# Splitting a crossbar transpose and reordering the steps of a fused attention and mixer kernel

## The chip, the cores and the metric

The kernel runs on one core of a Trainium2 chip. The metric is the device time of one execution in microseconds (us). A run is called slow when it took over 1.5% longer than the fastest of its kernel. A difference of up to 2% is called "same".

Engines are named as the profile names them: PE is TensorE (matmuls), PEld its weight loads, DVE is VectorE, ACT is ScalarE, POOL is GpSimd, SP is SyncE, which here only issues transfers.

## The reference, cut to what matters

Eight batches, eight heads, 576 positions, head size 64. Causal attention with a decay bias comes first. Its output x (batch, 576, 512) goes through a low-rank mixer over positions and a two-layer network over channels:

```python
scores = scale * q @ k.T + minimum(bias, 0)        # causal; bias from a cumulative sum of s
x  = softmax(scores) @ v                           # heads side by side: (8, 576, 512)
u  = x + ((x.T @ U) @ V).T                         # rank 32, over positions
out = u + relu(u @ w_ch1) @ w_ch2                  # 512 -> 2048 -> 512, each token alone
```

## The kernel before

Work is written down as strings of short tokens, played in order. Each engine gets its own instructions in that order, and they wait for one another by semaphores. Heads go in pairs; four pairs make a batch. Tokens are cut into nine groups of 512, which don't line up with the batches of 576 positions. Thus group 2 of the tokens needs the mixed x of pair 11, the last pair of batch 2.

The tokens that the argument needs:

| token | what it does |
|---|---|
| `F`, `e` | one feed step: four 512-column matmuls of the channel network (`e` only from pair 16 on); `r` runs what follows them on ACT or DVE |
| `D` `E` / `d` `f` `m` | score matmuls of a head / their exponentials on ACT |
| `A`, `a` | value matmuls of a head / division on DVE, which yields x |
| `x` | crossbar transpose of the x of one pair (SP) |
| `Y`, `y` | mixer matmuls of one pair / addition of turned x, on DVE, which yields uT, the input of the network |
| `G` | one vector transpose (DVE) of four heads' q or k; the second and the fourth of a head group also issue four copies to the score slots (SP) |
| `W` | crossbar transpose of u of token group 0; later groups are turned inside their feed steps |
| `p`, `Z` | filler matmuls on PE / memsets on DVE (`Z1`: of the third score slot) |
| `k0 v0 s0 ...` in LOADS | the first loads, in order of issue: a mask (`k`), v of a batch (`v`), q and k of heads (`s`, `q`), U and V of the mixer (`u0`, `u1`), pieces of w_ch1 (`w`) and of w_ch2 (`x`) |

A suffix such as `x-2@1` means: the step for the pair two back, only in pairs whose number is 1 modulo 4.

```python
    def turn_group(g):                   # token G
        ...
        nc.vector.transpose(turned[:, e, c]..., src[:, c]...)
        if c == 1:
            for a in range(4):
                nc.sync.dma_start(out=slots[...], in_=turned[...])      # "slot<-turned"

    def turn_x(n):                       # token x
        nc.sync.dma_start_transpose(
            out=xT[n % 3], in_=x_of[n // PB][:, n % PB].rearrange("p t c -> p (t c)"))

    def turn_u(g):                       # one transfer, 16 blocks of 128 columns
        nc.sync.dma_start_transpose(
            out=u_sb[g % 2].rearrange("p d i c -> p (d i) c"),
            in_=uT[:, g % 4].rearrange("p d c -> p (d c)"))

    def mix_done(copy, n):               # token y: "uT L461"
        ...
                    nc.vector.tensor_add(dst, got[:, p - lo : e - lo], turned[:, p:e])

    PAIR = (                             # played once for each pair from 8 on
        "G1 F U-1@1 F r F D0 uA-1@1 Y-5@1 r D1 e d0 Y-4@2 r r x-3@0 G1 E1 yA-5@2 l0 yA-4@2 d1 "
        "A-2 x-2@0 yV-5@1 k0 k1 A-1 e E0 Y-3@2 Y-4@1 f1 a-2 m1 e r f0 x-2@2 r F a-1 x-2@1 K0 r "
        "yA-3@2 m0 ")
```

Two lists stand beside this: `SEQ`, the steps up to pair 7 (here "the preamble"), and `BANKS`, the PSUM bank of each tile in order.

The softmax here doesn't subtract the row's maximum and nothing guards it: scores larger than these inputs give would overflow.

## Time and profile before

| what | before | where it is read |
|---|---|---|
| time, median (lowest to highest) | 376.36 us (375.08 to 378.12), 4 runs | the runs |
| span of the profiled execution | 373.5 us (time 375.49) | page |
| first feed step | 36.39 us | PE's timeline |
| first scores of pair 8 | 79.7 us | PE's timeline |
| idle of PE in 0 to 45, 45 to 80, 80 to 140 us | 5.05, 0.26, 7.63 us | summed over PE's timeline |
| DVE waiting for turned x | 9.4 us | waits by engine |

### The profile page before, as it was taken

To read this page: it belongs to the slowest core of one execution; us is meant where nothing else is said; L and a number is where in the kernel's file an instruction comes from. 1 tells how busy PE (TensorE), PEld (TensorE's weight loads), DVE (VectorE), ACT (ScalarE), POOL (GpSimd) and SP (SyncE) were. 2 spreads that over 40 slices of the span, in tenths; PEclk is the share of its full clock that TensorE was granted. 3 is DMA by queue.
4 is the path that set the end of the run, shared out by engine and by line. 5 is a ranking of instruction groups with operands and counts; after the bars stand their busy time and mean duration, and the time that the engine had idled before them with its cause. 6 is when DMAs were issued, how large, how long until landed. Compare 5 with 4: busy or idle time off the path is not lost.

```text
span 373.5 us, 7658 instructions
## 1 busy us (share of the span) xinstructions
PE 355.2 (95%) x2968; PEld 197.3 (53%) x3014; DVE 192.5 (52%) x410; ACT 206.9 (55%) x397; POOL 108.4 (29%) x177
## 2 busy tenths in 40 slices
PE   8898999998999499999999999999999999999995
PEld 4567565445565265555555555555554444444443
DVE  7689776665878365677547555744333111011011
ACT  7799894078664188546853677448812611612610
POOL 8838464546356356474090000000000000000000
PEclk9999999999999699999999999999999999999999
DMA  7999999999999999999999731371033203203102
GB/s 91 176 202 167 172 136 163 193 214 212 149 153 177 169 177 143 156 200 175 172 137 137 175 79 35 109 165 34 2 79 90 54 28 104 38 28 113 29 31 82
DMA packets 113979, 46.16 MB, mean 124 GB/s; under 512 B 98272, under 2 KB 105824, under 8 KB 113944
## 3 DMA queue, kind: packets, MB, share of 16 engines
q0 software_dynamic: 65760, 18.54, 60.7%
q1 hardware_dynamic: 48184, 27.14, 37.7%
q8 instruction: 23, 0.38, 0.5%
q14 instruction: 12, 0.10, 0.1%
HBM read 37.73 MB, written 10.03 MB: 128 GB/s over the span
## 4 chain that ended last, share of the span: by engine, by line
PE 77%; DMA 9%; DVE 7%; ACT 3%; issue 2%; SPq 1%; DVEq 0%
PE pwork L480 30%; PE pwork L500 30%; PE pscore L265 9%; PE pwork L344 5%; DMA slot<-turned 4%; DVE slot L236 3%; DMA stage<-x_sb 2%; DMA slot<-rows_hbm 2%; PE pwork L440 2%; ACT slot L236 1%; SPq L256 1%; DVE x_sb L360 1%; ACT pT L330 1%; DVE slot L573 1%; PE pwork L375 1%
## 5 line engine op out<-in xcount | busy, mean ns | idle before, releaser
L480 PE MATMUL pwork<-uT,w_sb 128*128 128x512 bf16 x552 | 132.8, 381 | 6.4 <-DVE uT L461 5.3
L330 ACT ACTIVATE pT<-pscore 128x512 bf16<-128x512 f32 (+1 forms) x224 | 110.5, 567 | 50.8 <-PE pscore L265 45.8
L487 ACT ACTIVATE hT<-pwork 128x512 bf16<-128x512 f32 x144 | 86.6, 606 | 83.0 <-PE pwork L480 80.7
L500 PE MATMUL pwork<-w_sb,hT 128*128 128x512 bf16 (+2 forms) x573 | 129.0, 373 | 1.6 <-DVE o_sb L513 0.6
L480 PEld LDWEIGHTS <-w_sb 128*128 128x128 bf16 x576 | 54.4, 98 | 64.8 <-issue 7.4
L500 PEld LDWEIGHTS <-hT 128*128 128x128 bf16 x592 | 55.6, 98 | 61.7 <-issue 1.9
L513 DVE TENSOR_TENSOR o_sb<-pwork,stage 128x512 f32<-128x512 f32 (+2 forms) x37 | 24.9, 674 | 98.0 <-PE pwork L500 94.8
L265 PE MATMUL pscore<-slot 128*128 128x128 bf16 (+4 forms) x576 | 63.0, 242 | 4.3 <-DVE slot L236 1.7
L265 PEld LDWEIGHTS <-slot 128*128 128x128 bf16 x576 | 41.1, 99 | 27.5 <-issue 4.3
L250 DVE STREAM_TRANSPOSE turned<-qk_sd 128x576 bf16<-128x576 bf16 x48 | 52.8, 1130 | 4.4 <-DMA qk_sd<-in_k_dram 4.0
L333 DVE TENSOR_TENSOR pT<-pT,keep 128x512 bf16<-128x512 bf16 (+1 forms) x84 | 28.3, 349 | 26.8 <-ACT pT L330 26.7
L138 POOL DMA_DIRECT2D qk_sd<-in_k_dram x48 | 27.1, 567 | 43.7 <-DMA v_slot<-in_v_dram 21.8
L461 DVE TENSOR_TENSOR uT<-pwork,stage 128x448 bf16<-128x448 f32 (+7 forms) x56 | 22.8, 448 | 31.5 <-PE pwork L440 22.1
L344 PE MATMUL pwork<-v_slot,pT 128*128 128x65 bf16 x960 | 35.0, 194 | 0.3 <-DVE uT L461 0.3
L138 POOL DMA_DIRECT2D qk_sd<-in_q_dram x48 | 27.2, 577 | 27.2 <-DVE uT L461 11.1
L344 PEld LDWEIGHTS <-pT 128*128 128x128 bf16 x960 | 33.5, 98 | 2.9 <-issue 0.6
L360 DVE TENSOR_TENSOR x_sb<-pwork,rec 128x320 bf16<-128x320 f32 x64 | 31.5, 491 | 2.2
L146 POOL DMA_DIRECT2D v_slot<-in_v_dram x32 | 28.2, 890 | 6.6 <-DMA qk_sd<-in_q_dram 2.6
L236 DVE COPY slot<-pwork 64x576 bf16<-64x576 bf16 x20 | 15.6, 797 | 4.3 <-PE pwork L224 3.9
L359 DVE RECIPROCAL rec<-pwork 128x5 f32<-128x5 f32 x64 | 11.8, 185 | 6.6 <-PE pwork L344 6.5
L440 PE MATMUL pwork<-V_sb,z_sb 128*128 128x64 bf16 (+7 forms) x63 | 12.6, 284 | 0.1
L560 PE MATMUL pwork<-warm 128*128 128x512 bf16 x34 | 10.3, 443 | 1.4 <-DVE warm L116 1.3
(77 smaller groups left out, 107.4 us busy)
## 6 DMA issues: line engine op xcount, KB each, us to landing
out_dram<-o_sb SPq DMA_DIRECT2D x35, 256.0 KB
slot<-turned SPq DMA_DIRECT2D x96, 72.0 KB
v_slot<-in_v_dram POOLq DMA_DIRECT2D x32, 128.0 KB, 7.9
w_sb<-in_moe_w_ch_dram POOLq DMA_DIRECT2D x8, 512.0 KB, 10.5
qk_sd<-in_q_dram POOLq DMA_DIRECT2D x48, 72.0 KB, 9.4
qk_sd<-in_k_dram POOLq DMA_DIRECT2D x48, 72.0 KB, 7.2
stage<-in_q_dram POOLq DMA_DIRECT2D x2, 288.0 KB, 8.6
stage<-in_k_dram POOLq DMA_DIRECT2D x2, 288.0 KB, 9.3
```

The source lines that it names most:

```text
L138: nc.gpsimd.dma_start(out=qk_t[g][ds(32 * a, 32), c, :].rearrange("p (n f) -> p n f", n=6), in_=src[g // 2, 4 * (g % 2) + a].rearrange("(n ...
L146: nc.gpsimd.dma_start(out=vt[:, t, :, 0:D], in_=v[b, :, ds(t * 128, 128), :].rearrange("h p d -> p h d"),)
L236: copy(dst[:, :, :, :, par], tp_of[h][par * D : par * D + D].rearrange("p c t m -> p c m t"),)
L250: nc.vector.transpose(turned[:, e, c].rearrange("p (n m t) -> p n t m", n=6, t=3), src[:, c].rearrange("p (n t e d) -> p e n t d", n=6, t= ...
L265: nc.tensor.matmul(dst, lhsT=head_of(h)[:, ds(S + j * 128, 128)], rhs=head_of(h)[:, lo:hi], start=start, stop=stop and not bias, skip_grou ...
L330: nc.scalar.activation(dst, src, EXP, scale=scale)
L333: nc.vector.tensor_tensor(p, p, m, op=ALU.min)
L344: nc.tensor.matmul(po[:, i, :], lhsT=p_of(h)[:, ds(spot(j, i), 128)], rhs=v_slots[h // H % 3][:, j, h % H, :], start=(j == 0), stop=(j == ...
L360: nc.vector.tensor_tensor(x_of[b][:, h % H // 2, :, ts(h % 2, D)], po[:, :, 0:D], rec.to_broadcast([128, 5, D]), op=ALU.mult,)
L480: nc.tensor.matmul(f1, lhsT=w1_sb[nf // 4][:, kt, ds(nf % 4 * 128, 128)], rhs=uT[:, g % 4, kt, :], start=(kt == 0), stop=(kt == 3),)
L487: pending.append(lambda nf=nf, f1=f1: nc.scalar.activation(hT[:, nf, :], f1, RELU))
L500: nc.tensor.matmul(f2[:, lo:hi], lhsT=hT[:, nf, ds(i * 128, 128)], rhs=w2_sb[nf // 4][:, nf % 4, lo:hi], start=(nf == 0), stop=nf == NF - ...
```

## The change

Its stated intent: u of a token group is turned by four crossbar transfers in place of one, x of batch 1 is issued ahead of u of group 0, and the steps of the main loop and the first loads stand in another order. It also assigns the banks anew. The diff, with the long strings cut:

```diff
-    def turn_u(g):
-        nc.sync.dma_start_transpose(
-            out=u_sb[g % 2].rearrange("p d i c -> p (d i) c"),
-            in_=uT[:, g % 4].rearrange("p d c -> p (d c)"),
-        )
+    def turn_u(g, d):
+        nc.sync.dma_start_transpose(out=u_sb[g % 2][:, d], in_=uT[:, g % 4, d])
     def widen(g):
-        if g > 0:
-            turn_u(g)
         for nf in range(NF):
+            if g > 0 and nf % 4 == 0:
+                turn_u(g, nf // 4)
-        "W": turn_u,
+        "W": lambda d: turn_u(0, d),
     LOADS = (
-        "k0 v0 s0 s1 w0 u0 w2 u1 w1 v1 x2 x0 q4 w3 x1 x3 q5 v2 "
+        "k0 s0 u1 v0 s1 u0 w1 q4 w0 v1 w2 w3 x0 x2 x1 x3 q5 v2 "
     SEQ = ( ... 11 lines anew: 27 feed steps in place of 35, 29 filler matmuls in place of 36 ... )
     PAIR = (
-        "G1 F U-1@1 F r F D0 uA-1@1 Y-5@1 r D1 e d0 Y-4@2 r r x-3@0 G1 E1 yA-5@2 l0 yA-4@2 d1 "
-        "A-2 x-2@0 yV-5@1 k0 k1 A-1 e E0 Y-3@2 Y-4@1 f1 a-2 m1 e r f0 x-2@2 r F a-1 x-2@1 K0 r "
-        "yA-3@2 m0 "
+        "F e r A-2 U-1@1 F r e D0 r E0 uV-1@1 d0 D1 d1 k0 x-3@1 l0 F f0 A-1 r a-2 Y-5@1 yA-5@1 "
+        "x-2@1 e K0 r m0 r x-3@0 F G1 x-3@3 E1 f1 r Y-4@2 F G1 a-1 r Y-4@1 Y-3@2 k1 yA-4@1 "
+        "yV-4@2 yV-3@2 m1 "
     BANKS = ( ... all anew ... )
```

Line numbers below the split fall by 3: L480, L500 and L513 of before are L477, L497 and L510 of after.

## The prediction

> **What bounds the kernel now.** I read the page's slices first, then the chain of waits, then TensorE's own timeline where the slices dip, then the SyncE queue.
>
> ```profile
> PE   8898999998999499999999999999999999999995
> ...
> PEclk9999999999999699999999999999999999999999
> DMA  7999999999999999999999731371033203203102
> ```
>
> TensorE (PE) is busy nearly everywhere. It has one hole, slice 14 (about 121 to 131 us), and in that slice the granted clock falls too. The 16 DMA engines are full from about 9 us to 205 us. So two limits lie over each other: matmul streaming sets the whole, and in the first third a transfer can still be late.
>
> ```profile
> 120.00:130.00 10.00, 4.73 (x22) 2.11 (x21) 4.36 (x9) 1.00 (x2) 2.83 (x5) 0.73 1.88 167
> ...
> 150.00:200.00 50.00, 49.63 (x457) 28.73 (x462) 30.96 (x67) 29.23 (x60) 23.54 (x37) 1.00 1.74 165
> 200.00:250.00 50.00, 49.63 (x444) 27.94 (x448) 30.84 (x68) 28.49 (x57) 0.00 (x0) 1.00 0.45 109
> 250.00:300.00 50.00, 49.63 (x373) 25.98 (x378) 16.71 (x45) 27.96 (x53) 0.00 (x0) 1.00 0.24 59
> 300.00:350.00 50.00, 49.79 (x229) 22.66 (x232) 5.53 (x8) 15.45 (x27) 0.00 (x0) 1.00 0.23 64
> ```
>
> These stretches (TensorE busy is the second number) show that from 150 us on there is nothing to take: 0.2 to 0.4 us idle in 50. What can be saved lies before 135 us.
>
> ```profile
> 119.73 1.67 PE L500 MATMUL pwork<-w_sb,hT 128*128 128x512 bf16 x7
> 121.24 0.81 PE L480 MATMUL pwork<-uT,w_sb 128*128 128x512 bf16 x3
> 127.32 2.29 PE L480 MATMUL pwork<-uT,w_sb 128*128 128x512 bf16 x5 [5.27 <-DVE uT L461]
> 129.41 2.02 PE L265 MATMUL pscore<-slot 128*128 128x128 bf16 x14
> ```
>
> The hole: 5.27 us of waiting for uT, then five matmuls that take 2.29 us. The chain of waits says why:
>
> ```profile
> 109.01 8.26 DMA slot<-turned
> ...
> 117.34 9.28 DMA stage<-x_sb
> ...
> 126.71 0.57 DVE uT L461
> ...
> 127.32 2.29 PE pwork L480 x5
> ```
>
> x of pair 11, turned by a crossbar DMA (stage<-x_sb), is issued only at 117.34, because SyncE first waited for a copy issued at 109.01, eight issues earlier on its queue; it then takes 9.28 us to land. Other waits of this kind (98.39 to 107.24, and V_sb issued at 20.79 behind a load issued at 12.58) also reach eight issues back, so I read the queue as holding eight transfers. When uT comes late, the matmul engine has no other work in program order: counting the feed steps in the program's strings, the step after the last add of batch 2 is the last of group 1 and the next is the first of group 2, which needs that add.
>
> ```profile
> 48.12 1.64 SPq L412 DMA_TRANSPOSE stage<-x_sb  x1
> 49.94 10.50 SPq L466 DMA_TRANSPOSE stage<-uT  x1
> 60.49 2.49 SPq L256 DMA_DIRECT2D slot<-turned  x4
> 63.15 4.88 SPq L412 DMA_TRANSPOSE stage<-x_sb  x3
> ```
>
> This is what the split of u aims at: one u transpose holds the SyncE queue for 10.50 us (5.85 and 5.43 for the next two), with head copies and x transposes behind it.
>
> **What the Trainium skill says.** "DMA: Bandwidth & Descriptors", section "Issuing engines are not separate DMA queues": all issuers share the same 16 DMA engines and interleave. The trace agrees: with them full, a 9.28 us landing cannot be bought off by a different issue order alone; it has to be issued earlier. The same page's rules ("Rules for kernel authors") advise issuing early and waiting late; the old order left 117.34 to 127.32 less 9.28 of it, that is nothing. The same page, "DMA Transpose (X-bar)", gives the form of the operation but no price for one against four; the trace must. "TensorE: Matmul & The Clock Gate", Part 1, says that the array falls to half clock after an idle window of about 3.4 us. The trace agrees: the granted clock was 0.73 in 120 to 130 us, and the matmuls after the hole start some 0.43 us apart, where warm ones start 0.216 us apart (4.32 us for 20 in the chain).
>
> **The change part by part.**
> *u in four.* Nine transposes become 36 (eight groups issued inside widening, group 0 by four tokens). In the quiet part an x transpose of five 128-column blocks holds SyncE 1.25 us, a u of sixteen 2.2, hence by the difference about 0.09 us a block and 0.8 fixed; a quarter is about 1.2 us and four are 4.7, my estimate. SyncE spends about 2.5 us more for each group, but never 5 to 10 in one piece. The bytes are unchanged. There are 27 more places taken in an eight-deep queue, mostly harmless after 200 us. Net on the path: 0, perhaps 1 us at pair 9, where two quarters, copies and outputs meet.
>
> *The main loop.* Feed steps (four 512-column matmuls, 0.863 us each) per pair go from 4 to 5 for pairs 8 to 15 and from 7 to 8 after; the preamble has 27 instead of 35; the tail 73 instead of 92. Work is only moved: the 8 steps taken from the preamble are 6.9 us, so pair 8 begins near 72.5 instead of 79.67, and pair 15 is level again. The point is the distance from x of pair 11 to the first step of group 2. Before: issue late in pair 13, then pair 14. After: issue in the middle of pair 13, pair 14 with five feeds, then two feeds, two value groups and scores first. With a pair at 5 x 0.863 + 0.92 (values) + 1.4 (scores), 6.6 us, that is about half of pair 13 with its mixing (4), pair 14 (7), and 3.4 in pair 15, some 14 us. Needed are 9.3 to land plus up to 2 or 3 on the queue. The wait of 5.27 should go. With it goes the cold clock: 5 matmuls at 2.29 instead of 1.08, and 2.02 instead of 1.10 for the score group of 14, together 2.1. Sum: 7.4 us.
>
> *Smaller waits before it.* TensorE lost 1.08 for slot<-turned at 91.49, 0.30 at 111.42 and 0.57 at 118.84 for uT, about 2. The new order moves the vector transposes that feed the copies to the last third of the pair, two together. From the second to the scores that use it I count one pair plus two feeds, some 9 us; the path needs 1.1 (transpose) + 1.2 (two copies issued) + 6.2 (landing at 85.06). It is tight, so I expect about 1 us saved and 1.5 new in pairs 9 to 14: net loss 0.5.
>
> *Opening.* Filler matmuls fall from 36 to 29, and the copies of turned heads go from 12 on ScalarE and 20 on VectorE to 10 and 22. ScalarE is full from 13 to 36 us (9.2 of 10 in 20 to 30), so batch 0 may be through 2 us sooner. But the first feed needs w0, which now stands behind s0, u1, v0, s1, u0, w1 and q4. From the trace's landings these took 6.0 (both s), 1.7, 5.9, 0.4, 3.4 and 2.9 us, w0 itself 3.5; from 12.74 this gives a landing at 36.5, where the first feed ran at 36.39 before. So most of that gain is stopped at w0. I count 0.5 us.
>
> Sum: 7.4 - 0.5 - 0 + 0.5 = 7.4 us, plus a little (0.6) because other gaps of the opening, 9 us in all beside ideal starts of matmuls up to 80 us, were searched over again in the new order. From 376.82 this gives 368.8.
>
> **Rivals.**
> (1) *The wait moves.* x of pair 9 is now issued two thirds into pair 12 for an add at the end of pair 13, about 9 us, the same as the landing; and the first vector transposes of group 6 come near 84 us, when its k loads landed only at 86.4. Either would stop VectorE for 1 to 3 us. For it: loads of groups 6 and 8 already made VectorE wait (2.8 and 1.3 us), and DMA is full. Against: TensorE has feeds that need none of this. If it reaches TensorE in each of pairs 9 to 14, 4 us go: 373.
> (2) *Weights come late.* If w0 or v0 lands 2 or 3 us later than summed, TensorE stands in the opening and maybe turns cold: 371. For it: v0 is put behind 4.7 us of other loads. Against: the old order reached its first values only at 22.25, with v0 there at 18.6.
> (3) *The opening really is faster.* If loads run denser and ScalarE is the only limit, the 2 us and the filler count: 366, with luck 364.
> (4) *The transfer is late anyway*, since eight places shared by more transposes keep x of pair 11 waiting: half of the hole stays, 372.
>
> **Range and chances.** The removal of the one large hole is well founded and worth just under 2%; opening and new small waits decide on which side of 2% (369.3) it ends. Range 364.0 to 373.5. Faster by over 2%: 0.53; within 2%: 0.44; slower by over 2%: 0.03, since after pair 16 only 0.2 in 50 us was idle and the same matmuls remain.
>
> **What would show it.** Right: no wait for uT above 1 us near the first step of group 2, the clock at 1.00 through 110 to 140, pair 8 starting at 71 to 74, SyncE issues of u near 1.2 us when quiet, the same 0.2 to 0.5 us idle in each 50 us after 150. Wrong: a TensorE wait above 2 us for slot<-turned, w_sb or v_slot; a first feed later than 38 us; VectorE stopped by qk_sd or stage<-x_sb for longer than a feed can cover; or a loop after pair 16 that waits for ScalarE or a bank.

## More of the kernel before

The waits by engine sum all idle time in front of one kind of instruction. The columns are the engine and the instruction, what it waited for, then us in total, times, longest. Of the kernel before:

```profile
PE pwork L480 <- DVE uT L461: 5.3, 1, 5.3
...
PE pscore L265 <- DMA slot<-turned: 1.1, 1, 1.1
...
DVE uT L461 <- DMA stage<-x_sb: 9.4, 4, 5.6
```

The one wait of 5.3 us is PE's hole. It stands for a DVE addition (uT), and DVE's own line says what that addition stood for: the crossbar transfer of x (stage<-x_sb), four times, 5.6 us at the worst. Follow such a pair of lines from the engine that bounds to the transfer.

## The result, and the profile after

After takes 371.0 us (median of 4 runs, 370.78 to 371.27) against 376.36 us. The ratio is 0.9855, with a 95% interval of 0.9812 to 0.9897. A ratio is the mean time of one kernel's fast runs over that of the other's fast runs of the same rounds, so it isn't quite the ratio of the medians quoted. By the 2% rule the two are the same, on the faster side. The profiled execution of after has a span of 369.5 us (time 371.17).

The page's slices after (40 slices of some 9.2 us: busy tenths of PE, granted clock, share of the DMA engines):

```profile
PE   8788999999999999999999999999999999999996
...
PEclk9899999999999999999999999999999999999999
DMA  7999999999999999999968973345114312203102
```

The dip at slice 14 is gone, in PE and in its clock. The second and third slices are a tenth lower than before, and in the second the clock is lower too. The DMA engines are full to about 185 us where they were full to 205, and partly busy for some slices longer. PE's waits after, as above:

```profile
PE pscore L265 <- ACT slot L236: 2.4, 2, 1.9
PE pwork L375 <- DVE x_sb L360: 1.4, 1, 1.4
...
PE pscore L265 <- DMA slot<-turned: 0.6, 1, 0.6
PE pwork L497 <- DMA w_sb<-in_moe_w_ch_dram: 0.5, 1, 0.5
```

There is no wait for uT any more, and no line in which DVE waits for stage<-x_sb to produce uT. The 2.4 and 1.4 us are new and lie in the opening.

Why the hole went is seen on SP. Its timeline after (start, duration, what was issued, how many in one piece):

```profile
112.05 4.13 SPq L412 DMA_TRANSPOSE stage<-x_sb  x2
116.28 0.43 SPq L173 DMA_DIRECT2D slot<-rows_hbm  x1
...
117.32 3.37 SPq L256 DMA_DIRECT2D slot<-turned  x4
```

The x of pair 11 is the second of the two at 112.05; it goes out near 114.6. The slot copies of the next head group follow it. Before, x stood behind four such copies:

```profile
113.85 3.23 SPq L256 DMA_DIRECT2D slot<-turned  x4
117.34 1.35 SPq L412 DMA_TRANSPOSE stage<-x_sb  x1
```

DVE now reaches the last addition of batch 2 without idling, and PE meets the first step of group 2 like this:

```profile
124.45 1.54 DVE L461 TENSOR_TENSOR uT<-pwork,stage 128x384 bf16<-128x384 f32 x4
```

```profile
125.27 1.10 PE L265 MATMUL pscore<-slot 128*128 128x128 bf16 x14
126.21 1.03 PE L477 MATMUL pwork<-uT,w_sb 128*128 128x512 bf16 x4
```

None of these lines ends in a bracket, so neither engine was idle ahead of them. The four matmuls take 1.03 us, at full clock; before, five took 2.29.

Where the rest went is seen in 10 to 20 us. The columns are the width, then busy us and instructions of PE, PEld, DVE, ACT and POOL, then the granted clock, the DMA share and GB/s. Before, then after:

```profile
10.00:20.00 10.00, 8.23 (x88) 5.67 (x89) 6.33 (x13) 7.39 (x14) 8.18 (x13) 1.00 1.83 179
```

```profile
10.00:20.00 10.00, 7.92 (x73) 5.34 (x74) 9.27 (x12) 4.29 (x8) 6.86 (x11) 0.83 1.54 182
```

DVE takes 9.27 us in place of 6.33 and ACT only 4.29 in place of 7.39. The first exponentials, before and then after, on ACT's timeline:

```profile
12.82 0.60 ACT L330 ACTIVATE pT<-pscore 128x512 bf16<-128x512 f32 x1 [2.40 <-PE pscore L274]
```

```profile
16.32 1.75 ACT L330 ACTIVATE pT<-pscore 128x512 bf16<-128x512 f32 x4 [3.80 <-PE pscore L285]
```

ACT starts its first exponentials 3.5 us later, and the first feed step runs at 40.41 us where it ran at 36.39.

The whole difference of the two profiled spans (373.5 - 369.5 = 4.0 us) can be split at the first scores of pair 8, if the feed steps that after leaves for later are booked where before did them. They are nine: the preamble has eight fewer, and ahead of these scores the new loop has two where the old one has three (9 x 0.863 = 7.8 us of PE):

| stretch | before | after | after, with the 7.8 us booked there | difference |
|---|---|---|---|---|
| start to pair 8's first scores | 79.7 | 77.1 | 84.9 | +5.2 |
| from there to the end | 293.8 | 292.4 | 284.6 | -9.2 |

The loop gained 9.2 us, nearly all of it the 7.0 us of idle time that went (7.63 to 0.64) and some 2.1 us of cold clock. The opening gave 5.2 back. Part of these 5.2 is chance: seven experiments below keep the order of steps of the old opening, some with other banks, and with the kernel before their first feed steps lie at 36.39, 37.8, 37.83, 38.1, 39.15, 39.52, 39.78 and 40.45 us. The profile of before is the earliest of the eight; their median is 38.6. The new opening, in five profiles (one of them with the old loads), gives 40.01 to 41.5, median 40.4. So at the first feed step the typical loss is nearer to 2 us than to 4. At pair 8's first scores, booked alike, it is 3.9: the median is 81.0 us in four fast profiles with all of the old preamble (before, b_x_early, b_x_first, h_sb_pa) and 84.9 in five with the new one. The 9.2 less 3.9 is close to the 5.4 us between the medians of the runs.

### The profile page after: what moved, and what is told of

Same layout as the page of the kernel before. It is cut to its first block, busy times and chain, and to the rows that moved or that the text cites.

```text
span 369.5 us, 7664 instructions
## 1 busy us (share of the span) xinstructions
PE 357.1 (97%) x3007; PEld 197.3 (53%) x3007; DVE 193.5 (52%) x416; ACT 203.3 (55%) x391; POOL 108.3 (29%) x177
## 4 chain that ended last, share of the span: by engine, by line
PE 77%; DMA 16%; POOL 4%; DVE 1%; issue 1%; ACT 0%; POOLq 0%
PE pwork L497 33%; PE pwork L477 28%; DMA w_sb<-in_moe_w_ch_dram 9%; PE pscore L265 8%; PE pwork L344 5%; DMA slot<-turned 3%; DMA stage<-in_k_dram 2%; DMA v_slot<-in_v_dram 2%; PE pwork L440 2%; POOL hT L120 1%; POOL v_slot L146 1%; DVE turned L250 1%; PE pwork L375 1%; POOL stage L127 1%; DVE o_sb L510 0%
## 5 line engine op out<-in xcount | busy, mean ns | idle before, releaser
L330 ACT ACTIVATE pT<-pscore 128x512 bf16<-128x512 f32 (+1 forms) x224 | 112.3, 558 | 86.7 <-PE pscore L265 78.5
L497 PE MATMUL pwork<-w_sb,hT 128*128 128x512 bf16 (+2 forms) x592 | 135.6, 373 | 1.2 <-DVE o_sb L510 0.6
L477 PE MATMUL pwork<-uT,w_sb 128*128 128x512 bf16 x576 | 135.0, 379 | 0.6 <-ACT hT L484 0.2
L497 PEld LDWEIGHTS <-hT 128*128 128x128 bf16 x592 | 54.9, 98 | 56.5 <-issue 2.2
L477 PEld LDWEIGHTS <-w_sb 128*128 128x128 bf16 x576 | 53.1, 98 | 56.7 <-issue 2.5
L265 PE MATMUL pscore<-slot 128*128 128x128 bf16 (+4 forms) x576 | 59.3, 241 | 3.9 <-ACT slot L236 2.4
L510 DVE TENSOR_TENSOR o_sb<-pwork,stage 128x512 f32<-128x512 f32 (+2 forms) x37 | 24.9, 672 | 58.8 <-PE pwork L497 58.2
L250 DVE STREAM_TRANSPOSE turned<-qk_sd 128x576 bf16<-128x576 bf16 x48 | 51.1, 1124 | 3.2 <-DMA qk_sd<-in_q_dram 2.1
L344 PEld LDWEIGHTS <-pT 128*128 128x128 bf16 x960 | 37.1, 98 | 13.6 <-issue 0.8
L344 PE MATMUL pwork<-v_slot,pT 128*128 128x65 bf16 x960 | 38.9, 193 | 0.5 <-ACT pT L330 0.3
L461 DVE TENSOR_TENSOR uT<-pwork,stage 128x448 bf16<-128x448 f32 (+7 forms) x56 | 22.5, 451 | 12.5 <-PE pwork L440 12.3
L236 DVE COPY slot<-pwork 64x576 bf16<-64x576 bf16 x22 | 17.3, 797 | 1.9 <-PE pwork L224 1.5
L395 DVE CAST z_sb<-pwork 128x512 bf16<-128x512 f32 x8 | 5.5, 688 | 17.2 <-PE pwork L384 17.2
L440 PE MATMUL pwork<-V_sb,z_sb 128*128 128x512 bf16 (+7 forms) x64 | 12.5, 286 | 0.0
```

The costliest lines, as they stand in the source:

```text
L250: nc.vector.transpose(turned[:, e, c].rearrange("p (n m t) -> p n t m", n=6, t=3), src[:, c].rearrange("p (n t e d) -> p e n t d", n=6, t= ...
L265: nc.tensor.matmul(dst, lhsT=head_of(h)[:, ds(S + j * 128, 128)], rhs=head_of(h)[:, lo:hi], start=start, stop=stop and not bias, skip_grou ...
L330: nc.scalar.activation(dst, src, EXP, scale=scale)
L344: nc.tensor.matmul(po[:, i, :], lhsT=p_of(h)[:, ds(spot(j, i), 128)], rhs=v_slots[h // H % 3][:, j, h % H, :], start=(j == 0), stop=(j == ...
L477: nc.tensor.matmul(f1, lhsT=w1_sb[nf // 4][:, kt, ds(nf % 4 * 128, 128)], rhs=uT[:, g % 4, kt, :], start=(kt == 0), stop=(kt == 3),)
L497: nc.tensor.matmul(f2[:, lo:hi], lhsT=hT[:, nf, ds(i * 128, 128)], rhs=w2_sb[nf // 4][:, nf % 4, lo:hi], start=(nf == 0), stop=nf == NF - ...
```

## The experiments

Three theories were to be told apart for the loop. **Split:** four short u transposes keep SP free, so x is issued in time. **Supply:** eight feed steps kept back give PE work until uT is there. **Order:** x stood behind slot copies in SP's in-order queue, and these waited for vector transposes; the new loop puts x ahead. For the opening the rivals were the order of the loads, the order of the copies and exponentials, and an early memset on DVE. Hybrids keep results right; where the number of steps changed, banks were dealt anew by one rule (the bank free for longest), which the last but one run checks. All twelve kernels gave right results.

### One part undone or done alone

**a_loads_old**: after, with the old order of loads.

```diff
-        "k0 s0 u1 v0 s1 u0 w1 q4 w0 v1 w2 w3 x0 x2 x1 x3 q5 v2 "
+        "k0 v0 s0 s1 w0 u0 w2 u1 w1 v1 x2 x0 q4 w3 x1 x3 q5 v2 "
```

> The changed kernel with the first loads in the old order. Theory L (load order cost the opening): the last w_sb piece lands near 61.6 us again instead of 68.2, the wait of 0.5 us for it goes, the first feed comes before 39 us instead of 40.4, and the time falls by 1.5 to 3 us, to 368 to 369.5. Rival O (the order of compute steps costs the opening, the loads were only there in time): first feed stays within 0.7 us of 40.4 and the time within 0.7 us of 371.0; since the vector transposes of group 4 stand early in the new order and q4 would land at 48.8, it may even be 1 to 2 us slower.

Measured: 371.63 us (370.78 to 373.48), ratio 0.9901 (0.985 to 0.9952). The first feed step stays at 40.41 us. The last w_sb lands at 63.2 us in place of 68.2, and the wait of 0.5 us for it goes; another, of 1.08 us for scores at 54.6, comes. So the order of the loads alone is worth nothing that can be seen, in either direction.

**a_u_one**: after, with u turned by one transfer, at the place of its first quarter.

```diff
-        nc.sync.dma_start_transpose(out=u_sb[g % 2][:, d], in_=uT[:, g % 4, d])
+        if d == 0:
+            nc.sync.dma_start_transpose(out=u_sb[g % 2].rearrange("p d i c -> p (d i) c"),
+                                        in_=uT[:, g % 4].rearrange("p d c -> p (d c)"))
```

> The changed kernel with u of a group turned by one crossbar DMA at its first quarter's place. Theory N (the split is nearly free and nearly useless by itself, because the hole went through a later demand, not a freer queue): 370.3 to 371.8, no wait of TensorE for uT above 1 us. Rival U (the split freed the SyncE queue and that closed the hole): u holds the queue 5 to 10 us again, x of pair 11 is issued 3 us or more later, a wait for uT of 2 to 5 us comes back, 373 to 376.

Measured: 370.55 us (369.96 to 371.34), ratio 0.9868 (0.982 to 0.9916). There is no hole; PE isn't idle right ahead of the first step of group 2. DVE does wait for x again, 3.2 us in three pieces (1.5 at the most), where it waits 0 in after: the quarters clear SP's queue for x as intended, but PE has other work at those places. **b_u_four** is the reverse: before, with u in quarters and nothing else.

```diff
-    def turn_u(g):                    # one transfer
+    def turn_u(g, d):                 # as in the change; widen() as in the change
-        "W": turn_u,
+        "W": lambda g: [turn_u(0, d) for d in range(4)],
```

> The kernel before with u in four quarters and nothing else (those of group 0 at one place). Theory N: the hole at 121 to 127 us stays within 1.5 us of 5.3, time within 1 us of before, 375.5 to 377.5. Rival U: the hole shrinks to under 2.5 us and the time falls by 3 us or more, to under 373.5.

Measured: 373.96 us (371.5 to 377.93), ratio 0.9949 (0.989 to 1.0007). Its profiled run was a slow one (377.93 us), so only its structure is read here, not its length:

```profile
130.58 1.93 PE L477 MATMUL pwork<-uT,w_sb 128*128 128x512 bf16 x5 [4.85 <-DVE uT L461]
```

The hole stands. The split theory falls as an explanation of the gain: without it the gain is all there, and with it alone the wait remains. A gain of up to 1% from the split in the old loop isn't excluded by the interval.

**a_z1_late**: after, with the memset on DVE (2.08 us at 12.37) moved behind the first copies of heads.

```diff
-... D0 tA2 E0 tV1 Z1 tV2 p2 D1 ... m0 tV7 f2 D5 tV8 ...
+... D0 tA2 E0 tV1 tV2 p2 D1 ... m0 tV7 f2 D5 Z1 tV8 ...
```

> The changed kernel with the 2.3 us of VectorE memsets of the third slot moved from just after the first head's copies to just before the slot's first use. Theory O1 (VectorE, 9.3 of 10 us busy between 10 and 20 us, is what delays the first exponentials, and the memset is the surplus): first feed 1 to 2.3 us earlier, time 369 to 370.3. Rival (another step of the order, exponentials of head 1 before head 0, sets it, or the loads do): first feed within 0.6 us of 40.4, time within 0.7 us of 371.0.

Measured: 371.17 us (370.6 to 374.42), ratio 0.9895 (0.984 to 0.9949). The first exponential comes at 14.67 us in place of 16.32, but PE then waits 2.59 us at 25.5, and the first feed step runs at 41.42, later than with the memset in its old place. The wait is for copies of heads on DVE, and what stands ahead of these copies is the memset itself, DVE's line first:

```profile
21.76 2.08 DVE L570 MEMSET slot<- 64x2432 uint32 x1 [0.55 <-issue]
```

```profile
25.53 0.82 PE L265 MATMUL pscore<-slot 128*128 128x448 bf16 x8 [2.59 <-DVE slot L236]
```

So the run moved the 2.08 us to another place on the path and didn't take them off it. It shows that this place is no better, and not that the memset costs the opening nothing.

### Two preambles, two loops

Four combinations: the preamble with 35 or 27 feed steps, the loop of before or of after. In these hybrids u is in one transfer where the preamble is the old one. **h_sb8_pb**: before, whose preamble lacks its last eight `F` and `r`.

```diff
-... r r Y7 R5 F r F F r F G5 L yA5 yV6 r F r r F F r yA7 r Q1 F F r G5 F r Q101 r F r
+... r r Y7 R5 F r F F r G5 L yA5 yV6 r yA7 Q1 G5 Q101
```

> The kernel before with nothing changed but this: the last eight feed steps of its preamble (and the eight follow steps that go with them) are left to the main loop, so 27 instead of 35 are done there; PSUM banks assigned anew, since every later allocation shifts. u whole, old loop, old loads. Theory S (the hole closes because eight feed steps are kept for later, so that group 2 is wanted later): no wait for uT above 1 us near 115 to 130 us, first feed still at 36.4, time 367.5 to 370. Rival P (the order of the loop, with x issued earlier beside it, closes the hole): a wait for uT of 3 us or more stays, time 374 or more.

**h_sb8_pa**: the same preamble and the loop of after. **h_sa_pb**: after, with the loop of before. **h_sb_pa**: before, with the loop of after.

```diff
 h_sb8_pa, against after
-    SEQ, LOADS of after; turn_u in quarters
+    SEQ of h_sb8_pb, LOADS of before; turn_u in one
 h_sa_pb, against after
-    PAIR of after
+    PAIR of before
 h_sb_pa, against before
-    PAIR of before
+    PAIR of after
```

> Preamble of before less its last eight feeds, old loads, u whole, main loop of the changed kernel. Theory S+O (the supply is what closed the hole, and the new preamble costs 4 us of opening): first feed 36.4, no hole, 366 to 369, faster than the changed kernel by 2 to 5 us. Rival (the late opening is hidden, because some load or later stage sets the pace anyway): within 1 us of the changed kernel's 371.

> The changed kernel with the old main loop (4 and 7 feeds a pair) and banks assigned anew. Theory S: the preamble alone, with its eight feeds fewer, closes the hole; 370 to 372.5, no wait for uT above 1 us. Rival P: a wait for uT of 3 us or more near 120 us, 374 to 377.

> The whole old preamble (35 feeds), old loads, u whole, and the new main loop with five feeds a pair. By count the loop wants 70 steps by the end of pair 14, and 64 exist before the last add of batch 2. Theory S: TensorE runs dry in pairs 13 and 14 and the wait for uT or for x_sb is as long as before or longer in sum, 375 to 380. Rival P: the new loop closes the hole whatever the supply, under 372.

| preamble, loop | time, median (range) | ratio (95%) | PE idle in 80 to 140 us | DVE waits for x to make uT |
|---|---|---|---|---|
| 35 feeds, old (before) | 376.36 | 1 | 7.63 | 9.4 |
| 27 feeds, old (h_sb8_pb) | 377.81 (374.19 to 381.47) | 1.0054 (0.9989 to 1.0119) | 5.91 | 7.4 |
| new preamble, old (h_sa_pb) | 382.08 (379.76 to 383.91) | 1.0172 (1.0116 to 1.0227) | 7.82 | 12.5 |
| 35 feeds, new (h_sb_pa) | 375.84 (373.64 to 377.7) | 1.0006 (0.9952 to 1.0061) | 5.76 | 1.4 |
| 27 feeds, new (h_sb8_pa) | 372.32 (370.01 to 374.48) | 0.9918 (0.9857 to 0.9978) | 0.79 | 2.2 |
| new preamble, new (after) | 371.0 (370.78 to 371.27) | 0.9855 (0.9812 to 0.9897) | 0.64 | 0 |

Ratios are to before (median 375.79 us). Kernels are compared only within the same rounds. By them h_sa_pb is unclear at the 2% rule, the others the same. The same is read from one line of each, busy time in 80 to 140 us (columns as before): h_sb8_pb, h_sb_pa and h_sb8_pa, in this order.

```profile
80.00:140.00 60.00, 54.09 (x592) 33.37 (x600) 41.80 (x90) 39.90 (x84) 37.21 (x59) 1.00 1.77 181
```

```profile
80.00:140.00 60.00, 54.24 (x554) 33.15 (x563) 38.60 (x86) 38.97 (x81) 35.68 (x56) 0.97 1.77 184
```

```profile
80.00:140.00 60.00, 59.21 (x577) 35.31 (x587) 40.72 (x89) 42.25 (x87) 34.40 (x54) 1.00 1.71 179
```

Supply alone (h_sb8_pb) removes the wait at the first step of group 2, but DVE goes on waiting for x, and PE now pays in other places: 2.71 us for uT at 110.4, 1.51 us for another product of DVE (o_sb) at 82.9. The new loop alone (h_sb_pa) frees DVE, but PE runs dry:

```profile
125.30 0.38 PE L480 MATMUL pwork<-uT,w_sb 128*128 128x512 bf16 x1 [3.39 <-DVE uT L461]
126.35 0.58 PE L480 MATMUL pwork<-uT,w_sb 128*128 128x512 bf16 x1 [0.68 <-DVE uT L461]
```

The new loop takes five feed steps for each pair up to pair 15 where the old one takes four. Counted in the strings, group 2 is asked for before its last addition unless the preamble leaves eight steps. With them (h_sb8_pa) the idle time in 80 to 140 us is nearly gone, with the old opening, the old loads and u in one piece. Just ahead of that stretch, at 77.4 us, PE does wait 3.05 us, for a vector transpose. So at this point two parts seemed to be needed: the new loop and the eight steps.

### The order of x alone

**b_x_early**: before, with one token moved.

```diff
-        "A-2 x-2@0 yV-5@1 k0 k1 ... r F a-1 x-2@1 K0 r "
+        "A-2 x-2@0 yV-5@1 x-2@1 k0 k1 ... r F a-1 K0 r "
```

> The kernel before with one token moved: the transpose of x of a batch's last pair is issued right after the add that frees its buffer, in the middle of pair 13, instead of near its end. Nothing else, same banks. Theory P' (the old loop leaves x too little time, and VectorE's wait for it is half of the hole): x of pair 11 issued 2 us or more before 117.3, VectorE's wait for it falls from 5.6 to under 3.5 us, the hole to under 3.5 us, time 1.5 to 4 us under before. Rival (the queue of eight holds it back anyway): issue within 1 us of 117.3, time within 1 us of before.

Measured: 375.35 us (375.09 to 377.15), ratio 0.9989 (0.9945 to 1.0032). SP's timeline, then PE's:

```profile
116.22 2.59 SPq L256 DMA_DIRECT2D slot<-turned  x4
118.91 1.26 SPq L412 DMA_TRANSPOSE stage<-x_sb  x1
```

```profile
129.51 2.29 PE L480 MATMUL pwork<-uT,w_sb 128*128 128x512 bf16 x5 [5.92 <-DVE uT L461]
```

The token was moved, and the transfer wasn't: it still stands behind the four slot copies of the second `G1`, which stands earlier in the string. The hole is 5.92 us. This says that nothing between those copies and the old place of x held it; it doesn't yet say that the copies did. That was left to the last run.

**best1**: an attempt at a better version than both: the old opening and loads without the eight steps, u in quarters spread, the vector transposes of group 4 earlier, the new loop.

```diff
-    SEQ, PAIR, turn_u of before
+    SEQ of h_sb8_pb with G4 moved ahead and W0 W1 W2 W3 apart; PAIR and turn_u of after
```

> The opening and the loads of the old kernel, with the eight last feeds of its preamble left out, vector transposes of group 4 moved ahead of the last feeds, u in quarters, and the loop of the changed kernel; old bank assignment up to the first dropped feed. Theory O (the new opening costs about 4 us that nothing later hides): first feed at 36.4 plus or minus 1, pair 8 before 74.5, no hole, 366.5 to 369. Rival: the second batch's v, landed near 79 us with these loads, is waited for in pair 9 and eats most of it, 369.5 to 371.5.

Measured: 376.62 us (375.67 to 380.07), ratio 1.0031 (0.9979 to 1.0082). It failed. PE waits 4.39 us at 81.4 for a uT of pair 7:

```profile
81.37 0.41 PE L265 MATMUL pscore<-slot 128*128 128x128 bf16 x5 [4.39 <-DVE uT L461]
```

The x of that pair was now issued only at 71.5 us. The opening in this profile was also the latest of the old ones (40.45 us).

**a_banks**: after, with banks dealt by the rule of the hybrids (473 of 541 changed).

```diff
-        "0123456712425637472537160135024510365...
+        "0123456712425673432573160157024710567...
```

> Control: the changed kernel with nothing changed but its PSUM banks, assigned by the same oldest-free rule as in the mixed kernels. If the mixed kernels can be compared with the changed one, this is within 1 us of 371; if it is slower by 3 us or more, the 382 us of the new preamble with the old loop is in part the banks' doing.

Measured: 370.31 us (369.84 to 371.54), ratio 0.985 (0.9804 to 0.9897), the same as after. So the rule by which the hybrids got their banks costs the changed kernel nothing, and it is unlikely to be what slowed h_sa_pb, whose own banks weren't varied.

**b_x_first**: before, with x moved as in b_x_early and the second `G1` (vector transposes and their slot copies) put right behind it. Supply, banks, loads, preamble and u stay as before.

```diff
-        "... r r x-3@0 G1 E1 yA-5@2 ... yV-5@1 k0 k1 ... r F a-1 x-2@1 K0 r "
+        "... r r x-3@0 E1 yA-5@2 ... yV-5@1 x-2@1 G1 k0 k1 ... r F a-1 K0 r "
```

> The kernel before with only the order of the steps of one pair of the loop changed: the crossbar transfer of the x of batch 1 stands right after the last y transpose of the same group, and the vector transposes and slot copies of the second head group stand right after that, where before they stood ahead of it. Banks as before, supply of feed steps as before. Theory (x of pair 11 stood behind slot copies in the in-order SyncE queue, and these waited for vector transposes): x of pair 11 is issued at 113.5 to 115 us instead of 117 to 119, VectorE's wait for it falls from 5.6 to under 2 or 3 us, the wait of TensorE for uT in pair 11 falls from 5.3 to under 2.5 us, and the time is 2 to 5 us under before. Rival (the depth of the queue of transfers holds it anyway): the transfer is issued within 1.5 us of where it was, the wait for uT stays at 4.5 us or more, and the time is within 1 us of before. A third reading, from the earlier runs of both loops and both supplies: the wait of VectorE goes, but TensorE still runs dry because the supply of feed steps is too short at that place, so that a gap of 3 us or more stays between 80 and 140 us.

Measured: 373.02 us (368.3 to 378.37, 6 runs), before 377.0 us (371.23 to 380.06, 11 runs). The ratio of the fast runs is 0.9923 (0.9799 to 1.0047), so the time is unclear. Two of its six runs and six of the eleven of before count as slow. Its profiled run is fast (372.38 us, span 368.9). SP's timeline, PE's, and DVE's waits:

```profile
115.30 1.26 SPq L412 DMA_TRANSPOSE stage<-x_sb  x1
117.47 2.66 SPq L256 DMA_DIRECT2D slot<-turned  x4
```

```profile
124.68 1.24 PE L480 MATMUL pwork<-uT,w_sb 128*128 128x512 bf16 x5 [0.61 <-DVE uT L461]
```

```profile
DVE uT L461 <- DMA stage<-x_sb: 1.6, 2, 1.0
```

x goes out at 115.30 us, copies behind it. DVE waits 1.6 us for x in all where it waited 9.4, the hole is 0.61 us, the clock is 1.00 from 80 to 140, and PE is idle 1.65 us there in place of 7.63. The third reading (dry supply) falls for the old loop: with four feed steps a pair the supply of before is enough once x is in time. The order theory holds, and it is the only one of the three that removes the hole alone and leaves no other in its place. In this profile the opening came out late (PE waits 1.74 us for V_sb at 35.52, first feed step at 39.78, pair 8 at 82.7). From pair 8 to the end it takes 368.9 - 82.7 = 286.2 us, where before took 293.8 and after, with its nine steps booked before pair 8, 284.6. What isn't shown is a gain in the runs' times that stands clear of their spread.

Two doubts can be settled from the traces. The first is what the copies ahead of x waited for. It was not the vector transposes, as the theory had it. In before the second transpose of that pair ended at 110.98 us:

```profile
109.83 1.15 DVE L250 STREAM_TRANSPOSE turned<-qk_sd 128x576 bf16<-128x576 bf16 x1 [1.25 <-DMA qk_sd<-in_k_dram]
```

The four copies went out at 113.85, 114.73, 115.79 and 116.58 us, each within 0.06 us of the landing of the transfer issued eight places before it (113.79, 114.71, 115.77 and 116.56), and x at 117.34 after a landing at 117.27. Of SP's 35 waits for transfers of its own in that profile, 32 are for the one eight places back. So every copy ahead of x makes x wait for one landing more. In b_x_first x stands four places earlier and waits in the same way (issued at 115.30, for a landing at 115.24). The depth of the queue, named as the rival, is thus part of the mechanism, and the order decides which landing x waits for. The buffer that x is written to isn't what held it before: DVE had freed it by 111.6 us.

The second doubt is that the late opening of this profile closed the hole by delaying PE. Counted from pair 8's first scores, x goes out after 37.7 us in before, 37.7 in b_x_early (whose opening was late by 1.6 us) and 32.6 in b_x_first, and PE reaches the first step of group 2 after 42.4, 42.4 and 41.4 us. A late opening moved both together; it was the order that brought x 5 us nearer.

## Why the prediction was right or wrong

The time was 368.8 us with a range of 364.0 to 373.5; measured were 371.0. The range holds it, and the class, within 2%, had a chance of 0.44. The gain was 5.4 us where 8.0 had been summed. Point by point:

1. **The hole and the cold clock after it, 7.4 us.** Right in cause and close in size. The idle time of PE in 80 to 140 us fell from 7.63 to 0.64, and the clock stayed at 1.00. Together with every other difference after pair 8's first scores, the loop gained 9.2 us. The mechanism is shown by b_x_first: the issue of x behind slot copies in SP's order, each of which waited for a landing eight places back. The prediction named the queue ("SyncE first waited for a copy issued at 109.01, eight issues earlier"); b_x_early showed that moving the token isn't enough while the copies are ahead of it. The slack of "nothing" that it found in the old order (117.34 to 127.32 less 9.28) is 0.70 us, the addition on DVE included.
2. **u in four, net 0.** Right. a_u_one (370.55 us) and after (371.0) are the same. A quarter holds SP 1.2 to 1.3 us where it is quiet, as estimated from the blocks, and 1.82 us at 54.60, where one whole had held it 10.50. In a_u_one DVE waits 3.2 us more for x, none of which reaches PE as a wait for uT, so it cleared the queue of nothing that the end waited for.
3. **Main loop: work only moved, pair 8 near 72.5 us.** The counting of feeds was right, and h_sb_pa shows that they matter to the new loop. The start of pair 8 was wrong: 77.1 us. The 79.67 is the time of its first scores, and ahead of those one feed step more has gone, nine (7.8 us) and not eight; against that sum the opening was 5.2 us late. The distance from the issue of x of pair 11 to the first step of group 2 was 11.6 us (114.57 to 126.21) where some 14 had been summed, and it was enough.
4. **Smaller waits, 0.5 us worse.** Too dark: 0.64 us idle remains in 80 to 140 us, one wait for slot<-turned at 103.86. The old order had about 2 us there besides the hole. The tight slack of the slot copies (one pair plus two feeds) held but for that.
5. **Opening, 0.5 us better, and 0.6 more for gaps "searched over again in the new order".** This is the step that failed, in sign. The first feed step comes at 40.4 us against 36.39 in the profile of before, and against a median of 38.6 over the old openings, so some 2 to 4 us were lost there, and 4 to 5 by pair 8's first scores, in place of 1.1 gained. The prediction had named a first feed later than 38 us as a sign of being wrong. The prediction had taken ScalarE as the limit from 13 to 36 us and the shorter list of copies on it as relief. In the trace ACT got less to do early because its input came later: DVE, with more head copies and the memset, was the busier engine in 10 to 20 us, and ACT idled 3.80 us ahead of its first exponentials. That this sets the first feed step isn't shown: in a_z1_late the exponentials came 1.65 us earlier and the step did not. It also took the time of one profile for the time of the opening, and that profile was the luckiest draw of eight.
6. **Rivals.** "The wait moves" did not come. "Weights come late" had the right size (371) but not the cause: w0 landed at 39.05 us, 2.5 later than summed, and v0 at 25.59, yet a_loads_old put the loads back and nothing moved. "The transfer is late anyway" did not come.

What stays open is the exact cause in the opening. The late copies, v0 and w0 fall together; a_loads_old shows that the order of the loads doesn't bind alone, and a_z1_late left the memset on the path. The half clock at 12 to 16 us isn't needed for it: a_banks and a_loads_old show a clock of 1.00 in 0 to 45 us, and their first feed steps came at 40.01 and 40.41. Also open is why the runs of before spread so far (371.23 to 380.06 beside b_x_first, where after, a_u_one and a_banks each stay within 1.7 us, a_loads_old within 2.7 and a_z1_late within 3.8). In four of the eight old openings PE waits for V_sb near 35 us, and that would fit, but only one execution of each kernel was traced.

## What to carry to other kernels

When an engine that only issues transfers works in order, ask for every late transfer what stands ahead of it there and what that waits for, here mostly a landing eight issues back: the edit that paid was to put the transfer that the bound waits for ahead of copies that had time. Splitting the transfers made no difference that the runs show, and keeping work in reserve helped only where that order was right. And read the start of a kernel from several executions before pricing a change there, since one profile can be the best draw.

## What the Trainium skill lacked or had wrong

- "DMA: Bandwidth & Descriptors", section "DMA Transpose (X-bar)": the section gives constraints but no price of issuing (the page's part on trn3 B0 has sequencer cycles for earlier generations, which no run here tests), and the page gives no number of transfers that one issuer can have under way. Here one transpose of 16 blocks held SyncE 1.86 to 2.67 us in quiet stretches and 5.43 to 10.50 with the DMA engines full; a quarter (four blocks) held it 1.2 to 1.3 quiet and 1.82 in a full stretch. Waits of SyncE for a landing reached eight issues back (32 of 35 in before; one of them 109.01 to 117.27 us), and the order of issue on it alone was worth a hole of 5.3 us, which fell to 0.61 in b_x_first.
- "TensorE: Matmul & The Clock Gate", Part 1: it names an idle window of about 3.4 us for the drop to half clock. In the profile of after the granted clock was 0.83 in 10 to 20 us, where PE was idle 2.08 us in all and 1.95 in one piece; the three other runs of after had a mean clock of 0.998 to 1.0. In a_banks, with a gap of 1.97 us at the same place, it stayed at 1.00 in 10 to 20 us. So with gaps shorter than the window the drop came in some executions and not in others.
